# Keys in chunks of 128 and a shared rest of 64: one change to an attention and SwiGLU kernel

## The chip, the cores and the metric

The kernel runs on one core of a Trainium2 chip. The metric is the device time of one execution in microseconds (us), the median of several runs. The engines are named as in the profile: PE is TensorE's matmul row and PEld its weight loads, DVE is VectorE, ACT is ScalarE, POOL is GpSimd, and SP is SyncE, which only issues transfers here.

## The reference

Attention over 8 batches of 12 heads, 448 tokens and head size 64 comes first. Its output, as 3584 tokens of 768 values, goes through a SwiGLU block with 1536 hidden values.

```python
scores = scale * np.matmul(q, k.transpose(0, 1, 3, 2))
attn = np.exp(scores - np.max(scores, axis=-1, keepdims=True))
attn = attn / (np.sum(attn, axis=-1, keepdims=True) + 1e-09)
x = np.matmul(attn, v).transpose(0, 2, 1, 3).reshape(B * S, H * D)
g = x @ w_gate
out = (g / (1.0 + np.exp(-g)) * (x @ w_val)) @ w_out
```

Inputs and output are float32. The kernel computes in float16 with float32 sums. It leaves the maximum out of the softmax, since the scores are small.

## The kernel before

**Attention, by pairs of heads.** There are 48 pairs. A pair's 448 keys lie as four chunks of 112 (P = 112, NC = 4). qk(pr, c) at L192 multiplies one chunk of transposed keys with all 448 queries, once for each head. The two matmuls use 64 rows each (the head size), and write the two halves of one buffer of the pool ps_s, which has three buffers. One exp on ACT (L205) turns the buffer into E, 112 x 896 in float16.

**Products, by two pairs.** Three products follow for every two pairs, that is four heads. sums(p0) (L236) multiplies E with ones and gives the row sums, and pv(p0, t) (L213) for t = 0 and 1 gives the two halves of the output values. Each product is 16 matmuls of 32 output columns: four chunks by four heads, one head in each quarter of the output rows. It needs one buffer of the pool ps_f, which has two. DVE empties that buffer: after sums by a copy to ssb (L255), with four reciprocals later (L258), and after pv by a multiplication with the reciprocals, which writes X (scaled, L232).

**FFN.** The tokens are cut into eight blocks of 384 and 512 in turn. ffn1_steps (L277) gives, for each of 12 slices of the hidden size, gp (a ps_s buffer, gate) and vp (a ps_f buffer, value), six matmuls each. ACT forms tanh of gp (L289), DVE forms t (L301) and then hts (L304), which frees vp. ffn2_steps (L309) gives op, 12 matmuls of 384 columns in a ps_f buffer for 128 tokens and half of the output. ACT copies op to osb (L334), and SP stores it. mm (L268) splits a matmul into four of 32 output columns while tiled is set, so that work beside a product has the same form as the product.

**The order around the change.** The whole order is written out by hand. After six pairs the loop over plan (L502) begins. Each visit has some score chunks (two up to pair 8, then three) and up to two due products. A visit issues its scores first, then the first product, then its share of the FFN (run_fv and run_o), with the second product before run_o or, in the first blocks, before all of the FFN share. Reciprocals wait in the list deferred and are issued one by one between FFN steps; a new product issues those that are left. Buffers of a pool are handed out in turn, and an instruction waits until the readers of the buffer it takes are done.

**Loads.** POOL issues the loads of q, k, v and the weights, which turn float32 into float16. load_qk16 (L112) brings two pairs, load_v (L121) three. From pair 11 on, prep (L144) copies a pair's q and k together on POOL (L154), and SP issues a transposing DMA (L157) into qkT. Earlier pairs are transposed on PE. Visits in which a pair begins call prep for the pair three ahead and load_qk16 for six ahead. wo, the output weights, are loaded in two halves by load_w, issued when pairs 6 and 7 begin.

Of the kernel before, what the change touches and what calls it, by code (L numbers as in the profile page):

```python
# [10 lines left out]
FP32 = mybir.dt.float32  # L11
# [10 lines left out]
RB = 5  # L22
FIRST = 6
TILED = 8
WIDE = 8


@with_exitstack
def kernel(
# [46 lines left out]
    ps_s = ctx.enter_context(tc.tile_pool(name="ps_s", bufs=3, space=PSUM))  # L76
    ps_f = ctx.enter_context(tc.tile_pool(name="ps_f", bufs=2, space=PSUM))

    ones = consts.tile([P, 32], FP16, name="ones")
    warm = consts.tile([128, 512], FP16, name="warm")  # L80
    ident = consts.tile([P, P], FP16, name="ident")
    wgv = {}
# [13 lines left out]
    E = {}  # L96
    R = {}
    X = {}

    def dummy(n):  # L100
        wp = ps_f.tile([128, 512], FP32, tag="f", name="wp")
# [9 lines left out]

    def load_qk16(pr, n=2):  # L112
        q16 = raws.tile([P, 4, NC, D], FP16, tag="rq", bufs=RB, name="q16")
        k16 = raws.tile([P, 4, NC, D], FP16, tag="rk", bufs=RB, name="k16")
        for dst, src in ((q16, q), (k16, k)):
            flat = src.rearrange("b h s d -> (b h) s d")[2 * pr : 2 * pr + 2 * n]
            nc.gpsimd.dma_start(dst[:, 0 : 2 * n], flat.rearrange("h (p c) d -> p h (c d)", c=NC))  # L117
        for i in range(n):
            raw[pr + i] = (q16[:, 2 * i : 2 * i + 2], k16[:, 2 * i : 2 * i + 2])

    def load_v(g, lo=0, hi=2 * GP):  # L121
        b = g // GPB
        h0 = (g % GPB) * 2 * GP
        if lo == 0:
            v16[g] = raws.tile([P, 2 * GP, NC, D], FP16, tag="vt", bufs=3, name="vt")
        nc.gpsimd.dma_start(  # L126
            v16[g][:, lo:hi],
            v[b, h0 + lo : h0 + hi].rearrange("h (p c) d -> p h (c d)", c=NC),
        )

    def load_w(kind, i):
        if kind == "o":
# [9 lines left out]
        nc.gpsimd.dma_start(dst[:], src)  # L142

    def prep(pr):  # L144
        rq, rk = raw[pr]
        if pr == 0 or pr >= NPE:
            qk16 = attp.tile([P, 2, NC, 2, D], FP16, tag="qk16", bufs=3)
            for t, src in enumerate((rq, rk)):
                dst = qk16[:, 1 - t].rearrange("p c h d -> p h c d")
                if pr == 0:  # L150
                    nc.vector.tensor_copy(dst[:, 0], src[:, 0])
                    nc.scalar.activation(dst[:, 1], src[:, 1], AF.Copy)
                else:
                    nc.gpsimd.tensor_copy(dst, src)  # L154
        qkT[pr] = attp.tile([128, 2 * NC, P], FP16, tag="qkT", name="qkT", bufs=5)
        if pr >= NPE:
            nc.sync.dma_start_transpose(  # L157
                qkT[pr][:], qk16[:].rearrange("p t c h d -> p (t c h d)")
            )
            return None  # L160

        def turn0():
            for t in range(2):
                tp = ps_s.tile([128, 2, 512], FP32, tag="s", name="tp")
                for c in range(NC):
                    for hx in range(2):
                        nc.tensor.matmul(
                            tp[ts(hx, 64), c // 2, ds(c % 2 * P, P)],
                            lhsT=qk16[:, 1 - t, c, hx],
                            rhs=ident[:],  # L170
                            start=True,
                            stop=True,
                        )
                dst = qkT[pr][:, ts(1 - t, NC)].rearrange("p (a c) q -> p a (c q)", a=2)
                nc.vector.tensor_copy(dst[:, 0], tp[:, 0, 0 : 2 * P])
                nc.scalar.activation(dst[:, 1], tp[:, 1, 0 : 2 * P], AF.Copy)

        def turn():
            if pr < FIRST + 2:
                tp = ps_s.tile([128, 2 * NC, 256], FP16, tag="s", name="tp")  # L180
            else:
                tp = ps_f.tile([128, 2 * NC, 128], FP16, tag="f", name="tp")
            for t in range(2):
                for c in range(NC):
                    for hx in range(2):
                        src = raw[pr][t][:, hx, c, :]
                        nc.tensor.transpose(tp[ts(hx, 64), (1 - t) * NC + c, 0:P], src, ident[:])
            nc.vector.tensor_copy(qkT[pr][:], tp[:, :, 0:P])

        return turn if pr else turn0  # L190

    def qk(pr, c):  # L192
        if c == 0:
            E[pr] = ep.tile([P, NC, 2, S], FP16, tag="E", name="E")
        t = qkT[pr]
        s = ps_s.tile([128, 2, 512], FP32, tag="s")
        for hx in range(2):
            nc.tensor.matmul(  # L198
                s[:, hx, 0:S],
                lhsT=t[ts(hx, 64)].rearrange("p c q -> p (c q)")[:, c * P : c * P + 128],  # L200
                rhs=t[ts(hx, 64), NC:, :].rearrange("p c q -> p (c q)"),
                start=True,
                stop=True,
            )
        nc.scalar.activation(E[pr][:, c], s[0:P, :, 0:S], AF.Exp, scale=sm_scale)  # L205

    def qk_half(pr, half, between=None):
        for c in (2 * half, 2 * half + 1):
# [1 line left out]
            if between and c % 2 == 0:  # L210
                between()

    def pv(p0, t):  # L213
        acc = ps_f.tile([128, 512], FP32, tag="f", name="acc")
        for c in range(NC):
            for j in range(4):
                g, r = divmod(p0 + j // 2, GP)
                nc.tensor.matmul(  # L218
                    acc[ts(j, 32), 0:S],
                    lhsT=v16[g][:, 2 * r + j % 2, c, :].rearrange("p (d t) -> p t d", t=2)[:, t],  # L220
                    rhs=E[p0 + j // 2][:, c, j % 2, :],
                    start=(c == 0),
                    stop=(c == NC - 1),
                )
        return acc

    def scaled(p0, t, acc):
# [8 lines left out]
    def sums(p0, wide=False):  # L236
        if wide:
            acc = ps_s.tile([128, 2, 512], FP32, tag="s", name="acc")[:, 0]
        else:
            acc = ps_f.tile([128, 512], FP32, tag="f", name="acc")  # L240
        for c in range(NC):
            for j in range(4):
                nc.tensor.matmul(  # L243
                    acc[ts(j, 32), 0:S],
                    lhsT=ones[:],
                    rhs=E[p0 + j // 2][:, c, j % 2, :],
                    start=(c == 0),
                    stop=(c == NC - 1),
                )
        R[p0] = attp.tile([128, S], FP32, tag="R", bufs=2, name="R")  # L250
        return acc

# [108 lines left out]
    with tc.manual_schedule():  # L361
        load_qk32(0)
        nc.vector.memset(warm[:], 0.0)
        nc.vector.memset(ones[:], 1.0)
        load_qk16(1, 1)
        make_identity(nc, ident)
        load_qk16(2, 1)
# [38 lines left out]
        def add_block(i, visits):  # L406
            f1, f2, n = block(i)
            oq.extend(ffn2_wait)
            ffn2_wait.clear()
            fvq.extend([(f1, NCB * n / 2400.0)] * NFB)  # L410
            own = [(f2, NFB * OH / 2400.0)] * (2 * (n // 128))
            (oq if i == 0 else ffn2_wait).extend(own)
            count.update(visits=visits, fv=NFB, o=len(oq), at=0, more=NFB - visits)
# [56 lines left out]
        load_table("exp_and_others")  # L470
        halves = [pv(p4, t) for t in range(2)]

        queue = []
        for p0 in range(FIRST, NPAIR, 2):
            for kind, m in (("sums", 8), (0, 11), (1, 14)):
                queue.append((NC * p0 + m, kind, p0))
        plan = []
        g = FIRST * NC
        last = NPAIR * NC
        while g < last or queue:  # L480
            n = 2 if g < WIDE * NC else 3
            todo = []
            while queue and queue[0][0] <= g and len(todo) < 2:
                todo.append(queue.pop(0))
            plan.append(([divmod(x, NC) for x in range(g, min(g + n, last))], todo))
            g += n
        adds = {0: 0}
        for x, (_, todo) in enumerate(plan):
            for _, kind, p0 in todo:
# [3 lines left out]
        def product(kind, p0):  # L493
            if kind == "sums":
                pop_deferred(99)
                deferred.extend(recips(p0, sums(p0)))
            else:
                pop_deferred(99)
                scaled(p0, kind, pv(p0, kind))

        carry = 0.0
        for x, (chunks, todo) in enumerate(plan):  # L502
# [9 lines left out]
            for pr in entered:  # L512
                if NPE <= pr + 3 < NPAIR:
                    prep(pr + 3)
                if pr % 2 == 0 and 14 <= pr + LA < NPAIR:
                    load_qk16(pr + LA)
                if (pr + 2) % GP == GP - 1 and 4 <= (pr + 2) // GP + 1 < NGRP:
                    load_v((pr + 2) // GP + 1)
            for pr, c in chunks:
                if c == 2 and pr < NPE - 2:  # L520
                    prep(pr + 2)()
            if todo:
                product(*todo[0][1:])
            if x in adds and x > 0:
                add_block(adds[x], end - x)
            for pr in entered:
                for w in wq.pop(pr, []):
                    emit(w)
            tiled[0] = bool(todo) and (not chunks or chunks[0][0] >= TILED)
            if adds[max(y for y in adds if y <= x)] < 2:  # L530
                for item in todo[1:]:
                    product(*item[1:])
# [55 lines left out]
```

## Time and profile before

| | us |
|---|---|
| median of 13 runs | 461.54 |
| lowest and highest run | 458.82 and 463.68 |
| the profiled execution, whole | 459.12 |
| its span, first to last instruction | 457.3 |
| busy time of the exps of the scores (L205) | 161.8 |
| busy time of POOL | 104.3 |

The profile shows one execution. Its busy times are those of that execution, and a sum made from them has to be set against 459.12, not against the median. Matmuls overlap each other, so the mean duration of one is longer than the distance from one start to the next; the distance between starts shows what PE needs. The granted clock of PE was 0.998 over the span. DMA is busy in nearly all of the first 80 us and much less after 120 us.

### The profile page before, as it was taken

The numbers are of one execution on the slowest core, as the hardware profiler recorded it, in microseconds if no ns is written. First come the engines' busy times: TensorE is split into PE (matmuls) and PEld (weight loads), VectorE is DVE, ScalarE is ACT, GpSimd is POOL, SyncE is SP. The second block draws the span as 40 slices with busy tenths as digits, with TensorE's granted clock in tenths as the row PEclk, the third lists the DMA queues.
The fourth block names the chain that finished last, engine by engine and source line by source line (L and its number), as shares of the span: only waits on it lengthen the run. The fifth ranks groups of instructions, "written<-read, shape, count | busy, mean of one in ns | idle before, by whom it ended". The sixth has DMA issues, their size and how long they took to land.

```text
span 457.3 us, 17024 instructions
## 1 busy us (share of the span) xinstructions
PE 448.2 (98%) x7807; PEld 249.6 (55%) x7807; DVE 239.2 (52%) x371; ACT 240.2 (53%) x353; POOL 104.3 (23%) x164
## 2 busy tenths in 40 slices
PE   8899999999999999999999999999999999999996
PEld 3355555444466665455566666555555666544564
DVE  2765764666764545745546546645466356354200
ACT  6986657666554655546364555544555551222222
POOL 8554704435160042301323013310200000000000
PEclk9999999999999999999999999999999999999999
DMA  9999999999984176940839358953222010100133
GB/s 135 195 200 201 184 179 165 149 198 138 105 106 64 43 110 101 151 83 9 127 61 129 57 79 128 120 51 76 33 57 56 20 54 20 56 0 1 36 103 105
DMA packets 82056, 44.42 MB, mean 97 GB/s; under 512 B 36672, under 2 KB 78528, under 8 KB 81984
## 3 DMA queue, kind: packets, MB, share of 16 engines
q0 software_dynamic: 42368, 23.37, 40.6%
q1 hardware_dynamic: 39520, 19.92, 25.4%
q8 instruction: 61, 1.00, 0.9%
q14 instruction: 11, 0.09, 0.1%
q10 hardware_dynamic: 96, 0.05, 0.0%
HBM read 47.19 MB, written 11.01 MB: 127 GB/s over the span
## 4 chain that ended last, share of the span: by engine, by line
PE 79%; DMA 14%; POOL 3%; DVE 2%; issue 1%; ACT 1%; POOLq 0%; DVEq 0%
PE gp L273 17%; PE vp L273 17%; PE op L273 15%; PE acc L218 7%; PE s L198 6%; PE op L270 6%; DMA q<-in_q_dram 6%; DMA wv<-in_moe_w_val_dram 5%; PE gp L270 4%; PE vp L270 4%; PE acc L243 3%; DMA wg<-in_moe_w_gate_dram 2%; DMA qkT<-qk 1%; POOL q L117 1%; POOL k L117 1%
## 5 line engine op out<-in xcount | busy, mean ns | idle before, releaser
L205 ACT ACTIVATE E<-s 112x896 f16<-112x896 f32 x192 | 161.8, 921 | 21.4 <-PE s L198 21.0
L273 PE MATMUL gp<-X,wg 128*32 128x384 f16 (+1 forms) x1848 | 100.7, 351 | 0.0
L273 PE MATMUL vp<-X,wv 128*32 128x384 f16 (+1 forms) x1848 | 100.5, 351 | 0.1
L301 DVE SCALAR_TENSOR_TENSOR t<-sg,gp 128x384 f32<-128x384 f32 (+1 forms) x96 | 59.1, 616 | 78.7 <-ACT sg L289 78.7
L289 ACT ACTIVATE sg<-gp 128x384 f32<-128x384 f32 (+1 forms) x96 | 52.8, 550 | 71.1 <-PE gp L273 45.7
L334 ACT ACTIVATE osb<-op 128x384 f32<-128x384 f32 (+1 forms) x57 | 27.7, 485 | 117.7 <-PE op L273 93.9
L273 PE MATMUL op<-wo,hts 128*32 128x384 f16 x1968 | 87.1, 326 | 0.8 <-DMA wo<-in_moe_w_out_dram 0.6
L273 PEld LDWEIGHTS <-wg 128*32 128x32 f16 x1848 | 53.0, 96 | 35.6 <-issue 0.2
L258 DVE RECIPROCAL R<-ssb 128x112 f32<-128x112 f32 x92 | 71.9, 822 | 0.8
L273 PEld LDWEIGHTS <-wv 128*32 128x32 f16 x1848 | 52.9, 97 | 33.8 <-issue 0.3
L273 PEld LDWEIGHTS <-hts 128*32 128x32 f16 x1968 | 56.9, 97 | 26.1 <-DMA wo<-in_moe_w_out_dram 1.0
L304 DVE SCALAR_TENSOR_TENSOR hts<-t,vp 128x384 f16<-128x384 f32 (+1 forms) x96 | 59.6, 621 | 10.4 <-DVE t L301 0.5
L232 DVE TENSOR_TENSOR X<-acc,R 128x448 f16<-128x448 f32 x48 | 29.7, 624 | 56.8 <-PE acc L218 53.7
L198 PE MATMUL s<-qkT 64*128 64x448 f16 x384 | 50.4, 353 | 2.8 <-ACT E L205 1.5
L126 POOL DMA_DIRECT2D vt<-in_v_dram x16 | 12.3, 772 | 157.7 <-PE acc L218 156.6
L218 PE MATMUL acc<-E,vt 112*32 112x448 f16 x768 | 45.1, 355 | 0.0
L154 POOL COPY qk<-q 112x512 f16<-112x512 f16 x37 | 22.9, 619 | 47.6 <-DMA qkT<-qk 28.7
L198 PEld LDWEIGHTS <-qkT 64*128 64x128 f16 x384 | 14.9, 94 | 33.3 <-issue 26.3
L255 DVE COPY ssb<-acc 128x448 f32<-128x448 f32 x23 | 14.4, 624 | 32.3 <-PE acc L243 32.2
L270 PE MATMUL op<-wo,hts 128*128 128x384 f16 (+1 forms) x192 | 29.6, 316 | 0.0
L218 PEld LDWEIGHTS <-vt 112*32 112x32 f16 x768 | 16.6, 96 | 23.3 <-issue 14.7
L270 PE MATMUL gp<-X,wg 128*128 128x512 f16 (+1 forms) x114 | 25.5, 360 | 0.0
(38 smaller groups left out, 204.7 us busy)
## 6 DMA issues: line engine op xcount, KB each, us to landing
vt<-in_v_dram POOLq DMA_DIRECT2D x16, 336.0 KB, 7.5
q<-in_q_dram POOLq DMA_DIRECT2D x22, 224.0 KB, 7.3
k<-in_k_dram POOLq DMA_DIRECT2D x22, 224.0 KB, 8.4
out_dram<-osb SPq DMA_DIRECT2D x7, 336.0 KB, 3.1
wg<-in_moe_w_gate_dram POOLq DMA_DIRECT2D x8, 288.0 KB, 11.3
wv<-in_moe_w_val_dram POOLq DMA_DIRECT2D x8, 288.0 KB, 11.5
wo<-in_moe_w_out_dram POOLq DMA_DIRECT2D x2, 1152.0 KB, 22.8
out_dram<-osb SPq DMA_DIRECT2D x8, 288.0 KB, 3.0
```

The costliest lines, as they stand in the source:

```text
L154: nc.gpsimd.tensor_copy(dst, src)
L198: nc.tensor.matmul(s[:, hx, 0:S], lhsT=t[ts(hx, 64)].rearrange("p c q -> p (c q)")[:, c * P : c * P + 128], rhs=t[ts(hx, 64), NC:, :].rear ...
L205: nc.scalar.activation(E[pr][:, c], s[0:P, :, 0:S], AF.Exp, scale=sm_scale)
L218: nc.tensor.matmul(acc[ts(j, 32), 0:S], lhsT=v16[g][:, 2 * r + j % 2, c, :].rearrange("p (d t) -> p t d", t=2)[:, t], rhs=E[p0 + j // 2][: ...
L232: nc.vector.tensor_tensor(X[kk][:, hp + t, ts(bb, S)], acc[:, 0:S], R[p0][:], ALU.mult)
L258: lambda i=i: nc.vector.reciprocal(rt[:, ts(i, P)], ssb[:, ts(i, P)]) for i in range(4)
L270: nc.tensor.matmul(dst, lhsT=lhsT, rhs=rhs, start=start, stop=stop)
L273: nc.tensor.matmul(dst[ts(j, 32), :], lhsT=lhsT[:, ts(j, 32)], rhs=rhs, start=start, stop=stop)
L289: nc.scalar.activation(sg[:, 0:n], gp[:, 0:n], AF.Tanh, scale=0.5)
L301: nc.vector.scalar_tensor_tensor(t1[:, 0:n], sg[:, 0:n], 1.0, gp[:, 0:n], ALU.add, ALU.mult)
L304: nc.vector.scalar_tensor_tensor(hts[:, fb, 0:n], t1[:, 0:n], 0.5 * HS, vp[:, 0:n], ALU.mult, ALU.mult)
L334: nc.scalar.activation(osb[:, ds(m0, w)], op[:, 0:w], AF.Copy, scale=1.0 / HS)
```

## The change

From pair 12 on (FULL = 12) a pair's keys and values lie as three chunks of 128 and a rest of 64. The rests of the two heads lie below each other on 128 partitions. For the scores, the rests of the keys are placed in a block-diagonal tile (the other blocks are set to zero), so that one matmul over 128 rows gives the rest scores of both heads, in one buffer of ps_f, with one exp of 448 elements. In the products the fourth step of each head reads this shared rest, with values, or ones, that are zero in the rows of the other head. The number of matmuls in a product stays 16.

The loads follow: k of two pairs takes three DMAs instead of one, v of three pairs takes three and a memset, and prep has two memsets and four copies instead of two copies. load_v is issued after the visit's first product.

The plan of visits changes. Visits have two chunks up to pair 8 and three from pair 9; from pair 12 on a visit is one pair, with its rest after the first product. Products are due by visits. Where a block's last product falls in a visit, all products due are issued at once, ahead of the rest.

```diff
-WIDE = 8
+FULL = 12
-    ones = consts.tile([P, 32], FP16, name="ones")
+    ones = consts.tile([128, 3, 32], FP16, name="ones")
...
     def load_qk16(pr, n=2):
...
+        km = k16[:, 0 : 4 * 3 * D].rearrange("p (h c d) -> p h c d", h=4, c=3)
+        kr = k16[:, 4 * 3 * D : 4 * 3 * D + 2 * D].rearrange("p (i d) -> p i d", i=2)
+        nc.gpsimd.dma_start(km, kf[:, 0:SM].rearrange("h (p c) d -> p h (c d)", c=3))
+        for hx in range(2):
+            nc.gpsimd.dma_start(
+                kr[ts(hx, SR)], kf[:, SM:].rearrange("(i t) p d -> t p i d", t=2)[hx]
+            )
...
     def load_v(g):
...
+        nc.gpsimd.memset(v_rest(g), 0.0)
+        nc.gpsimd.dma_start(v_main(g), v[b, heads, 0:SM].rearrange("h (p c) d -> p h (c d)", c=3))
+        for hx in range(2):
+            nc.gpsimd.dma_start(
+                v_rest(g)[ts(hx, SR), :, hx],
+                v[b, heads, SM:].rearrange("(i t) p d -> t p i d", t=2)[hx],
+            )
...
     def prep(pr):
+        if pr >= FULL:
+            rq, km, kr = raw[pr]
+            qk16 = attp.tile([128, 2, NC, 2, D], FP16, tag="qk16", bufs=3, name="qk16")
+            nc.gpsimd.memset(qk16[96:128, 1], 0.0)
+            nc.gpsimd.memset(qk16[:, 0, 3], 0.0)
+            nc.gpsimd.tensor_copy(qk16[:, 0, 0:3].rearrange("p c h d -> p h c d"), km)
+            for hx in range(2):
+                nc.gpsimd.tensor_copy(qk16[ts(hx, SR), 0, 3, hx], kr[ts(hx, SR)])
+            nc.gpsimd.tensor_copy(qk16[0:P, 1].rearrange("p c h d -> p h c d"), rq)
+            qkT[pr] = attp.tile([128, 2 * NC, 128], FP16, tag="qkT", name="qkT", bufs=5)
+            nc.sync.dma_start_transpose(
+                qkT[pr][:], qk16[:].rearrange("p t c h d -> p (t c h d)")
+            )
+            return None
...
     def qk(pr, c):
...
+        m = 128 if full else P
+        dst = (e_main if full else e_old)(pr)[:, c]
+        nc.scalar.activation(dst, s[0:m, :, 0:S], AF.Exp, scale=sm_scale)
+
+    def qk_rest(pr):
+        s = ps_f.tile([128, 512], FP32, tag="f", name="sr")
+        mm(s[:, 0:S], lhsT=qkT[pr][:, 3], rhs=qkT[pr][:, NC:, 0:P], start=True, stop=True)
+        nc.scalar.activation(e_rest(pr), s[:, 0:S], AF.Exp, scale=sm_scale)
...
+    def reduce4(p0, acc, weights):
         for c in range(NC):
             for j in range(4):
-                g, r = divmod(p0 + j // 2, GP)
+                pr, hx = p0 + j // 2, j % 2
+                if pr < FULL:
+                    rhs = e_old(pr)[:, c, hx, :]
+                else:
+                    rhs = e_main(pr)[:, c, hx, :] if c < 3 else e_rest(pr)
                 nc.tensor.matmul(
                     acc[ts(j, 32), 0:S],
-                    lhsT=v16[g][:, 2 * r + j % 2, c, :].rearrange("p (d t) -> p t d", t=2)[:, t],
-                    rhs=E[p0 + j // 2][:, c, j % 2, :],
+                    lhsT=weights(pr, hx, c),
+                    rhs=rhs,
                     start=(c == 0),
                     stop=(c == NC - 1),
                 )
...
+        nc.vector.memset(ones[:, 0], 1.0)
+        for hx in range(2):
+            nc.vector.memset(ones[:, 1 + hx], 0.0)
+            nc.vector.memset(ones[ts(hx, SR), 1 + hx], 1.0)
...
+        visits = []
+        g = FIRST * NC
+        while g < FULL * NC:
+            n = 2 if g < 9 * NC else 3
+            visits.append([divmod(x, NC) for x in range(g, g + n)])
+            g += n
+        visits += [[(pr, c) for c in range(3)] for pr in range(FULL, NPAIR)]
+        done = {pr: x for x, chunks in enumerate(visits) for pr, _ in chunks}
+        plan = []
         queue = []
         for p0 in range(FIRST, NPAIR, 2):
-            for kind, m in (("sums", 8), (0, 11), (1, 14)):
-                queue.append((NC * p0 + m, kind, p0))
+            x = done[p0 + 1] + 1
+            step = 2 if x < len(visits) and len(visits[x]) == 2 else 1
+            queue += [(x, "sums", p0), (x + step, 0, p0), (x + step + 1, 1, p0)]
...
-            if todo:
+            if x in adds and x > 0:
+                while todo:
+                    product(*todo.pop(0)[1:])
+                add_block(adds[x], end - x)
+            elif todo:
                 product(*todo[0][1:])
-            if x in adds and x > 0:
-                add_block(adds[x], end - x)
             for pr in entered:
+                if (pr + 2) % GP == GP - 1 and 4 <= (pr + 2) // GP + 1 < NGRP:
+                    load_v((pr + 2) // GP + 1)
                 for w in wq.pop(pr, []):
                     emit(w)
-            tiled[0] = bool(todo) and (not chunks or chunks[0][0] >= TILED)
+            tiled[0] = bool(todo or x in adds) and (not chunks or chunks[0][0] >= TILED)
+            for pr in entered:
+                if pr >= FULL:
+                    qk_rest(pr)
```

## The prediction

> **What bounds the kernel now.** I read the page first, then the waits, then stretches of the timeline by engine.
>
> ```profile
> PE 448.2 (98%) x7807; PEld 249.6 (55%) x7807; DVE 239.2 (52%) x371; ACT 240.2 (53%) x353; POOL 104.3 (23%) x164
> L205 ACT ACTIVATE E<-s 112x896 f16<-112x896 f32 x192 | 161.8, 921 | 21.4 <-PE s L198 21.0
> ```
>
> TensorE is busy for 98% of the span; ScalarE, the engine that the change relieves, for 53%. So the time follows from what TensorE streams and from its gaps. The waits give one gap for each entry into the score matmuls (73 of them):
>
> ```profile
> PEld L198 <- issue: 26.3, 73, 0.7
> ```
>
> The timeline of PE alone, one visit (a turn of the loop over plan, numbered x from 0 below) of block 1, shows what an entry costs:
>
> ```profile
> 97.19 0.74 PE L198 MATMUL s<-qkT 64*128 64x448 f16 x6
> 97.86 0.94 PE L243 MATMUL acc<-E,ones 112*32 112x448 f16 x16
> 98.63 1.47 PE L273 MATMUL gp<-X,wg 128*32 128x512 f16 x24
> 99.92 1.47 PE L273 MATMUL vp<-X,wv 128*32 128x512 f16 x24
> 101.22 1.47 PE L273 MATMUL gp<-X,wg 128*32 128x512 f16 x24
> 102.51 1.47 PE L273 MATMUL vp<-X,wv 128*32 128x512 f16 x24
> 103.91 0.36 PE L198 MATMUL s<-qkT 64*128 64x448 f16 x2
> ```
>
> Starts matter here, not durations. Six groups of four 32-column matmuls take 1.295 us (99.92 to 101.22), 0.216 per 512 columns; by columns, 0.189 for 448 and 0.1625 for 384. Into the scores 102.51 to 103.91 is 1.40, so 0.105 is lost; out of them 97.19 to 97.86 is 0.67 for three chunks of 0.189, so 0.10 is lost. Product to gp is 0.77 for 0.756. Nothing else is lost: all waste beside these 0.205 us a visit is a real wait, as here:
>
> ```profile
> 130.18 1.16 PE L273 MATMUL vp<-X,wv 128*32 128x384 f16 x24
> 131.16 0.94 PE L243 MATMUL acc<-E,ones 112*32 112x448 f16 x16
> 131.59 0.55 DVE L304 SCALAR_TENSOR_TENSOR hts<-t,vp 128x384 f16<-128x384 f32 x1
> 132.20 2.13 PE L273 MATMUL op<-wo,hts 128*32 128x384 f16 x48
> ```
>
> acc to op takes 1.04 for 0.756 of columns: op needs the ps_f buffer (of two) that vp held, and VectorE gives it back at 132.14. A product's buffer comes back later still:
>
> ```profile
> 210.18 0.94 PE L218 MATMUL acc<-E,vt 112*32 112x448 f16 x16
> 211.17 0.62 DVE L232 TENSOR_TENSOR X<-acc,R 128x448 f16<-128x448 f32 x1 [1.70 <-PE acc L218]
> ```
>
> It is free 0.99 + 0.62 + about 0.07 = 1.68 us after the product's start. Last, the DMA limits two places:
>
> ```profile
> 63.30 0.94 PE L218 MATMUL acc<-E,vt 112*32 112x448 f16 x16
> 64.79 1.49 PE L273 MATMUL op<-wo,hts 128*32 128x384 f16 x32 [0.55 <-DMA wo<-in_moe_w_out_dram]
> ```
>
> ```profile
> 48.37 25.27 DMA q<-in_q_dram
> ...
> 75.50 5.88 DMA qkT<-qk
> 81.39 0.05 issue
> 81.43 0.74 PE s L198 x6
> ```
>
> The first op waits 0.73 us for w_out (1.49 less 0.756), and pair 14's scores at 81.43 follow its transposing DMA (the second fence is the chain of waits in 55 to 85 us).
>
> [...] the key and value rests write 128 B runs, which no row of before shows.
>
> **The change, part by part.**
>
> *Columns.* A pair before is 4 score chunks, after 3 chunks and a rest: the rest streams 448 columns once, like a chunk. Products keep 16 matmuls of 448. FFN work is the same. Net 0. Memsets of ones at the start: under 0.1 us each (L364 has 85 ns), beside the first loads, 0.
>
> *ScalarE.* Per pair 4 exps at 921 become 3 and one of 448 (L264, 448 wide, has 577 ns): 36 x 0.34 = 12 us less, worth 0 by itself, as TensorE is the bound. But tanh now queues behind four exps: in the stretch above it started at +2.96 us after the scores (100.15), and will at about +3.5.
>
> *Visits.* From the instruction order: visits with scores go from 58 to 46, since 8 chunks of two pairs took 2.67 visits and now take 2. 12 x 0.205 = -2.5. The rest sits between product and gp, which hides the 0.02 that gp waited there: 36 x 0.02 = -0.7. Third chunks waited 0.01 each, 24 fewer: -0.2.
>
> *w_out.* With pair 8 now in visits of two, op in visit x=8 comes after 2 chunks and one product less: 0.38 + 0.76 = 1.1 us of columns wait for later, while w_out sets the start at 64.8 as before. The key load of pair 12 is ahead of it in the queue: 512 + 256 packets instead of 448. Taking 50 and 32 ns each (on a line through the trace's median packets, 512 B at 60 and 768 B at 79 ns) and 16 engines, +0.44 us; between 0 and 1.5, as short packets are not shown. Together +1.6 (0.5, if something else already holds the visits before it, to 2.6).
>
> *Pair 14's scores.* They come at visit x=12, which by the sums here is about 85 us instead of 81.4. Its keys land some 1 to 2 us later (w_out, own packets), and POOL's queue issues four DMAs a load, each waiting for the one eight earlier, so pair 16's load, queued ahead of pair 14's copies, waits for 14's own; then two memsets and four copies (0.62 per 512 columns, so about 2.2 us instead of 1.2) and 5.9 to landing: 85.3 to 86.2. +0.9 (0 to 2.5). Later pairs are prepared three visits (about 24 us) ahead; POOL at some 4.5 us a pair stays covered, and so does SP, whose transposes stand behind out stores only. load_v moved behind the visit's first product: POOL waits for that product, and what is queued behind (the pair three on) has over two visits; 0.
>
> *The rest takes a ps_f buffer, and two buffers rotate.* Product in A, rest in B, so what follows next needs A, free at +1.68.
> - x=10, 14, 16: a second product follows; 1.68 - 0.756 - 0.189 = 0.73 each, +2.2. At x=10 op then needs B, held until the rest's exp ends at about +3.5 from the scores while op is ready at 3.1: +0.45 (0 to 0.6).
> - x=11: op follows the rest: +0.73.
> - x=12, 18, 24, 30, 36, 42: two products ahead of the rest, 1.68 - 2 x 0.756 = 0.16: +1.0.
> - x=20, 22, 32, 34, 44 (384 columns) and 26, 28, 38, 40 (512): sums after two vp, then op, as at 131.16: 5 x 0.29 + 4 x 0.36 = +2.9 (1.8 to 4); the 0.36 adds the longer L304 and the earlier end of vp. Visit 46 has one more, +0.3.
> - x=13, 15, 17: the third chunk needs gp's buffer, which VectorE reads late after the later tanh: +0.5 (0 to 1). At 103.91 before it fitted by 0.05.
>
> *Waits of before that go:* 0.17 at 81.4, two of 0.29 (132, 241), 0.42 at 352 to 354, small ones of about 0.5: -1.4.
>
> Sum: -3.4 + 1.6 + 0.9 + 2.65 + 0.7 + 1.0 + 3.2 + 0.5 - 1.4 = +5.8. The profiled execution took 459.12 us (span 457.3 and 1.8 around it), so 464.9 of that kind; it is 2.4 us below the median of the 13 runs, so 461.54 + 5.8 = 467.3.
>
> **Rivals.**
> - *The rotation costs little, and the kernel gets faster.* Place: the ps_f waits above, 8.1 us in all with the third chunks. If VectorE and ScalarE free buffers as early as TensorE asks, 5.8 - 8.1 = -2.3: 459.2. It decides once these waits come to under about 0.9 us (the rest of the sum is -2.3, and 1.4 can be told apart). For it: most ps_f hand-overs of before cost nothing. Against: 131.16 to 132.20 shows the very sequence, and 1.68 against 0.95 is not close.
> - *No change.* The 12 mode changes and the waits cancel, with w_out no later and the sums waits half: 461.5. Against: each wait has its own row.
> - *The loads lag.* 128 B and 384 B runs cost far more than I take, and POOL's chain of eight holds each later load; pairs 14 to 18 come late by 4 to 6 us more: 472. For it: DMA share is over 1.3 until 80 us. Against: it falls to 0.3 to 0.9 from 120 us.
>
> **How the numbers follow.** Forecast (463 to 469.5) 0.64, loads lag 0.14, no change 0.12, faster 0.10. This kernel's runs tell 0.3% (1.4 us) apart. Slower 0.78, same 0.12, faster 0.10. The range leaves out part of the faster case and the upper end of the lag: 461 to 471.
>
> **What would show it.** Right: 61 issue gaps instead of 73; first op near 65 us with 2 to 3 us of wait; a second product 1.7 us after the first at three visits; op 0.3 late after sums in nine visits; the last score matmul's visit later than before. Wrong: sr followed at once by acc or op, or a wait on DMA qkT in many visits.

## The result, and the profile after

The kernel after takes 465.38 us, median of 11 runs (462.34 to 467.89); the kernel before takes 461.35 in 48 runs beside them. The ratio is 1.0096, with a 95% interval of 1.0073 to 1.012: 4.4 us more (461.35 x 0.0096). The profiled execution of after took 465.38 us, its span 463.6, which is 6.3 us above the 457.3 of before.

The page of after, engines first, then the instruction queue and the row of the score exps:

```profile
PE 448.7 (97%) x7843; PEld 247.5 (53%) x7843; DVE 239.1 (52%) x375; ACT 226.1 (49%) x353; POOL 184.7 (40%) x380
...
q8 instruction: 61, 1.00, 0.9%
...
L263 ACT ACTIVATE E<-s 128x896 f16<-128x896 f32 (+1 forms) x156 | 131.4, 923 | 12.8 <-PE s L260 12.6
```

ScalarE lost 14.1 us of work (240.2 to 226.1), and POOL got 80.4 more (104.3 to 184.7). TensorE's busy time is nearly the same (448.2 and 448.7), and so the time follows from its gaps. The waits of after:

```profile
PEld L260 <- issue: 21.8, 61, 0.7
...
POOL vt L156 <- DMA wo<-in_moe_w_out_dram: 3.6, 1, 3.6
...
PE op L350 <- issue: 2.3, 1, 2.3
...
PE acc L284 <- DVE X L311: 1.7, 3, 0.6
...
PE vp L350 <- issue: 0.8, 1, 0.8
...
PE op L350 <- DVE hts L381: 0.7, 4, 0.2
```

There are 61 entries into the scores instead of 73. The three waits of a product for X are the three second products of the prediction. What it did not have are the two waits of matmuls on "issue", that is, waits for nothing that the profile shows. The timeline of PE around a second product (visit 14), around a visit in which op follows sums (visit 20), and at the first op (columns: start, duration, what, and in brackets the idle time before it):

```profile
97.47 0.94 PE L284 MATMUL acc<-E,vt 128*32 128x448 f16 x16
98.23 0.36 PE L350 MATMUL sr<-qkT 128*32 128x448 f16 x4
99.14 0.94 PE L284 MATMUL acc<-E,ones 128*32 128x448 f16 x16 [0.54 <-DVE X L311]
```

```profile
149.12 0.93 PE L284 MATMUL acc<-E,ones 128*32 128x448 f16 x16
150.17 1.16 PE L350 MATMUL op<-wo,hts 128*32 128x384 f16 x24
```

```profile
61.80 0.94 PE L284 MATMUL acc<-E,ones 112*32 112x448 f16 x16
62.56 1.64 PE L350 MATMUL op<-wo,hts 128*32 128x384 f16 x36
```

From 97.47 to 99.14 is 1.67 us for 0.945 of columns: 0.72 lost. From 149.12 to 150.17 is 1.05 for 0.756: 0.29 lost. At 61.80 to 62.56 nothing is lost (0.76 for 0.756); the wait for w_out that before had there is gone.

The new gap, in the timeline of PE and in windows of one microsecond (busy share of PE, PEld, DVE, ACT and POOL with counts, then granted clock, DMA share, GB/s):

```profile
285.75 3.10 PE L350 MATMUL op<-wo,hts 128*32 128x384 f16 x72
291.18 1.78 PE L350 MATMUL op<-wo,hts 128*32 128x384 f16 x24 [2.33 <-issue]
292.90 1.30 PE L260 MATMUL s<-qkT 64*128 64x448 f16 x6
294.13 1.33 PE L284 MATMUL acc<-E,vt 128*32 128x448 f16 x16
295.30 0.93 PE L284 MATMUL acc<-E,ones 128*32 128x448 f16 x16
```

```profile
289.00:290.00 1.00, 0.00 (x0) 0.00 (x0) 0.00 (x0) 0.00 (x0) 0.00 (x0) 1.00 0.03 1
290.00:291.00 1.00, 0.00 (x0) 0.00 (x0) 0.00 (x0) 0.00 (x0) 0.00 (x0) 1.00 0.01 0
...
293.00:294.00 1.00, 1.00 (x6) 0.18 (x5) 0.00 (x0) 0.99 (x2) 0.00 (x0) 0.50 0.00 0
```

In the middle of op's matmuls every engine stands still, and then TensorE runs at half clock: 292.90 to 295.30 takes 2.40 us for two groups that need 0.67 and 0.756. The gap costs 2.5 us, the slow stretch some 1.6; a smaller one of 0.93 lies at 247.7. Before's profiled execution has one such gap, of 0.1 us, at 301.08. What is it that TensorE has none of? The DMA view of after for 278.2 to 288.6 us and for 288.6 to 291.2 (queue, packets, MB, share of 16 engines):

```profile
q0 software_dynamic: 1241, 0.45, 45.0%
q1 hardware_dynamic: 1156, 0.65, 39.8%
```

```profile
q0 software_dynamic: 39, 0.00, 3.1%
q8 instruction: 1, 0.02, 3.0%
q1 hardware_dynamic: 60, 0.01, 2.5%
```

The queue "instruction" (q8) moves TensorE's program, going by the count: 61 packets for 2 x 7843 matmuls and weight loads are 257 instructions each, 61 for 2 x 7807 in before are 256, and 30 for 2 x 3847 in e5 below are 256 again. So a packet is read here as a block of 256 instructions. Matmuls of a quarter width and 384 columns start every 0.1625 / 4 = 0.041 us and have a weight load each, so a block lasts about 128 x 0.041 = 5.2 us, an estimate from these starts. Through the 10.4 us from 278.2 to 288.6, two blocks long, a burst of stores, loads and a transposing DMA ran and no packet of q8 came (one of q14, the other instruction queue, did). The packet came as the burst ended, and TensorE, dry since about 288.6, went on at 291.18.

That these gaps stand between two blocks can be counted. Two windows of after run from the start of the span into the two gaps:

```profile
0.00:248.60 248.60, 240.58 (x4444) 129.73 (x4444) 142.39 (x226) 145.06 (x216) 149.70 (x302) 1.00 0.98 131
0.00:290.00 290.00, 280.45 (x5339) 154.01 (x5340) 163.19 (x260) 163.46 (x247) 166.19 (x338) 1.00 0.94 125
```

Matmuls and weight loads together are 8888 and 10,679. These are 1791 apart, and with one semaphore instruction of TensorE between them, which the windows leave out, 1792, which is seven times 256. e3 and e6 below show the same distances at other places of the work.

### The profile page after: what moved, and what is told of

It reads as the page before. It is cut to its first block, busy times and chain, and to the rows that moved or that the text cites. A ratio compares the mean times of both kernels' runs of the same rounds, so it can differ in the third digit from the quotient of the medians.

```text
span 463.6 us, 17335 instructions
## 1 busy us (share of the span) xinstructions
PE 448.7 (97%) x7843; PEld 247.5 (53%) x7843; DVE 239.1 (52%) x375; ACT 226.1 (49%) x353; POOL 184.7 (40%) x380
## 4 chain that ended last, share of the span: by engine, by line
PE 88%; DVE 5%; ACT 3%; issue 1%; DMA 1%; SPq 0%; DVEq 0%; ACTq 0%
PE gp L350 18%; PE op L350 18%; PE vp L350 16%; PE acc L284 11%; PE s L260 7%; PE op L347 6%; PE gp L347 5%; PE vp L347 5%; ACT E L263 2%; DVE t L378 2%; PE sr L350 2%; DVE hts L381 1%; ACT sg L366 1%; DVE R L335 1%; DMA rk<-in_k_dram 1%
## 5 line engine op out<-in xcount | busy, mean ns | idle before, releaser
L263 ACT ACTIVATE E<-s 128x896 f16<-128x896 f32 (+1 forms) x156 | 131.4, 923 | 12.8 <-PE s L260 12.6
L350 PE MATMUL vp<-X,wv 128*32 128x384 f16 (+1 forms) x1824 | 99.5, 351 | 0.8 <-issue 0.8
L350 PE MATMUL gp<-X,wg 128*32 128x384 f16 (+1 forms) x1824 | 99.2, 351 | 0.0
L350 PE MATMUL op<-wo,hts 128*32 128x384 f16 x1968 | 87.2, 328 | 4.4 <-issue 2.3
L350 PEld LDWEIGHTS <-hts 128*32 128x32 f16 x1968 | 56.1, 97 | 32.7 <-issue 7.8
L350 PEld LDWEIGHTS <-wv 128*32 128x32 f16 x1824 | 50.4, 97 | 36.4 <-issue 1.1
L350 PEld LDWEIGHTS <-wg 128*32 128x32 f16 x1824 | 50.8, 97 | 34.6
L153 POOL MEMSET vt<- 128x384 f16 x12 | 5.0, 418 | 114.4 <-PE acc L284 114.4
L284 PE MATMUL acc<-E,vt 128*32 128x448 f16 (+1 forms) x768 | 45.6, 357 | 0.2 <-DMA vt<-in_v_dram 0.2
L260 PE MATMUL s<-qkT 64*128 64x448 f16 x312 | 41.9, 357 | 2.1 <-ACT E L263 1.5
L284 PEld LDWEIGHTS <-vt 128*32 128x32 f16 (+1 forms) x768 | 16.9, 97 | 23.9 <-issue 15.3
L347 PE MATMUL op<-wo,hts 128*128 128x384 f16 (+1 forms) x192 | 29.6, 316 | 0.0
L347 PE MATMUL gp<-X,wg 128*128 128x512 f16 (+1 forms) x120 | 26.7, 358 | 0.2 <-DVE t L378 0.2
L260 PEld LDWEIGHTS <-qkT 64*128 64x128 f16 x312 | 12.2, 94 | 27.3 <-issue 21.8
L347 PE MATMUL vp<-X,wv 128*128 128x512 f16 (+1 forms) x120 | 26.6, 358 | 0.0
L284 PE MATMUL acc<-E,ones 128*32 128x448 f16 (+1 forms) x384 | 22.6, 353 | 2.1 <-DVE X L311 1.7
```

The lines of the kernel that those rows point to most:

```text
L153: nc.gpsimd.memset(v_rest(g), 0.0)
L260: nc.tensor.matmul(s[:, hx, 0:S], lhsT=lhsT, rhs=rhs, start=True, stop=True)
L263: nc.scalar.activation(dst, s[0:m, :, 0:S], AF.Exp, scale=sm_scale)
L284: nc.tensor.matmul(acc[ts(j, 32), 0:S], lhsT=weights(pr, hx, c), rhs=rhs, start=(c == 0), stop=(c == NC - 1),)
L347: nc.tensor.matmul(dst, lhsT=lhsT, rhs=rhs, start=start, stop=stop)
L350: nc.tensor.matmul(dst[ts(j, 32), :], lhsT=lhsT[:, ts(j, 32)], rhs=rhs, start=start, stop=stop)
```

## The experiments

Two theories stood against each other. W: the 4.4 us are the waits of the prediction, ps_f above all. F: they are mostly late instruction packets, and the rotation (the two buffers of ps_f, taken in turn) is a lesser part. Each comparison uses runs of before on the same chip in the same hour; before's median moved there between 459.5 and 461.7.

**e1: products first.** After, with all due products ahead of the rest, so that the rest no longer takes the buffer of the second one.

```diff
-            if x in adds and x > 0:
+            had = bool(todo)
+            if (x in adds and x > 0) or (chunks and chunks[0][0] >= FULL):
                 while todo:
                     product(*todo.pop(0)[1:])
-                add_block(adds[x], end - x)
             elif todo:
                 product(*todo[0][1:])
+            if x in adds and x > 0:
+                add_block(adds[x], end - x)
```

> The changed kernel with every product that is due issued ahead of the rest from pair 12 on (all work kept). Theory W (the extra time is mostly waits for the two rotating ps_f buffers): three waits of 0.74 before a second product become 0.15 before the rest, nine waits of 0.28 to 0.34 before op become 0.15 before the rest, the wait of op at x=10 stays at 0.4 to 0.5: 3.1 us less than the changed kernel, about 462.3 median. Theory F (the extra time is mostly TensorE running out of instructions, the gaps that the trace calls issue): the same waits vanish from the trace, but the median stays above 464, since the gaps of 1 to 2.5 us stay.

Measured: 461.34 us (22 runs) against 461.26; ratio 1.0017 (0.9998 to 1.0035). The same visit in the timeline of PE:

```profile
97.02 0.94 PE L284 MATMUL acc<-E,vt 128*32 128x448 f16 x16
97.79 0.93 PE L284 MATMUL acc<-E,ones 128*32 128x448 f16 x16
98.69 0.37 PE L350 MATMUL sr<-qkT 128*32 128x448 f16 x4
98.88 1.48 PE L350 MATMUL gp<-X,wg 128*32 128x512 f16 x24
```

The 0.72 between the products is gone, and 0.14 comes ahead of the rest (97.79 to 98.69 is 0.90). The order of the products is worth some 4 us (3.6 by the two ratios), 3.1 of which W priced. F, which expected more than 464, misses here too. Gaps on issue of 1.1 and 1.4 us are still there in the profiled execution. So W's waits are real, and they aren't all that the change brought.

**e2: no rest loads.** After, without the DMAs of the key and value rests; these rests count as zero, so the last 64 keys of each head enter with scores and values of zero.

```diff
-        for hx in range(2):
-            nc.gpsimd.dma_start(
-                kr[ts(hx, SR)], kf[:, SM:].rearrange("(i t) p d -> t p i d", t=2)[hx]
-            )
+        nc.gpsimd.memset(kr, 0.0)
...
         nc.gpsimd.dma_start(v_main(g), v[b, heads, 0:SM].rearrange("h (p c) d -> p h (c d)", c=3))
-        for hx in range(2):
-            nc.gpsimd.dma_start(
-                v_rest(g)[ts(hx, SR), :, hx],
-                v[b, heads, SM:].rearrange("(i t) p d -> t p i d", t=2)[hx],
-            )
```

> The changed kernel without the loads of the rests of k and v (their rows are zero instead, so part of the attention is left out); TensorE, ACT and DVE do what they did. 36 + 24 DMAs and 9,200 packets of 128 B are gone. Theory W: no change against the changed kernel, 465.4 within 0.6 us. Theory F, with short packets delaying the fetch of instructions: 1.5 to 3 us less, 462.4 to 463.9, and fewer gaps called issue.

Measured: 462.89 us (11 runs), ratio 1.004 (1.0018 to 1.0061), 2.5 us below after. The instruction sequence of TensorE is that of after, and its ps_f waits stayed (2.2 us before second products, as in after). The gaps on issue shrank to 0.6 and 0.2 us, without half clock. W alone, which expected no change, falls. And the wait for w_out is back, in the timeline of PE:

```profile
62.21 0.94 PE L276 MATMUL acc<-E,ones 112*32 112x448 f16 x16
64.52 1.80 PE L342 MATMUL op<-wo,hts 128*32 128x384 f16 x39 [1.37 <-DMA wo<-in_moe_w_out_dram]
```

The two profiles agree with the time: fetch gaps and half clock take 0.8 us here and 5.0 in after (2.5 + 1.6 + 0.93), and the wait for w_out adds 1.55 (64.52 less 62.21, less 0.756), which makes 2.65 us less.

**e3: short runs in before.** Before, with the keys and values from pair 12 on loaded in two DMAs of 256 B runs each instead of one of 512 B: 16,608 more packets and 30 more DMAs.

```diff
+            for e in range(2):
+                nc.gpsimd.dma_start(dst[:, 0 : 2 * n, ts(e, 2)], flat[:, :, ts(e, 2 * D)])
...
+        for e in range(2):
+            nc.gpsimd.dma_start(v16[g][:, lo:hi, ts(e, 2)], src[:, :, ts(e, 2 * D)])
```

> The kernel before, with k and v from pair 12 on loaded by two DMAs each in runs of 256 B instead of 512 B (same bytes and results, 16,000 packets more, 30 DMAs more). Theory F, with short packets delaying the fetch of instructions: 1.5 to 3 us slower than before, with gaps called issue of 1 us or more in the trace. Theory W: the same as before within 0.6 us.

Measured: 461.26 us (22 runs), as before itself; ratio 0.9995 (0.9975 to 1.0016). A miss for F as it stood then: more and shorter packets do not by themselves move the median. The kernel isn't free of late fetches, though. Its profiled execution, one of its longest (463.18 us), has gaps on issue of 0.6, 1.1 and 0.7 us: in a product, ahead of gp and in op. Counted as above, they stand behind 2495, 2751 and 10,687 instructions, which is 1 and 31 blocks of 256 apart. Before has runs as long (up to 463.92 us), but none of those was profiled, so whether such gaps make them long is not shown.

**e4: half an exp in before.** Before, with half of the fourth chunk's exp from pair 12 on left out; the second head's part is set to one by POOL.

```diff
-        nc.scalar.activation(E[pr][:, c], s[0:P, :, 0:S], AF.Exp, scale=sm_scale)
+        w = 1 if pr >= 12 and c == 3 else 2
+        nc.scalar.activation(E[pr][:, c, 0:w], s[0:P, 0:w, 0:S], AF.Exp, scale=sm_scale)
+        if w == 1:
+            nc.gpsimd.memset(E[pr][:, c, 1], 1.0)
```

> The kernel before, with the exp of the fourth chunk done for one of two heads only from pair 12 on (36 times 0.34 us less on ScalarE; the other half of E is set to one by POOL, so this part of the computation is left out). Both theories: ScalarE is not the bound, so the same as before within 0.6 us. A rival in which ScalarE's work is on the path says up to 12 us less.

Measured: 460.4 us (22 runs) against 461.26; ratio 1.0002 (0.9979 to 1.0025), so the same, with ScalarE at 228.5 us instead of 240.2. The relief that the change brings to ScalarE is worth nothing, as the prediction had it.

**e5: fewer instructions.** After, with the FFN's matmuls at full width (only the rest stays split in four): 3847 matmuls instead of 7843.

```diff
-TILED = 8
+TILED = 99
...
             for pr in entered:
                 if pr >= FULL:
+                    tiled[0] = True
                     qk_rest(pr)
+                    tiled[0] = False
```

> The changed kernel with the FFN matmuls left whole in every visit (128 output columns, not four times 32), so that TensorE has 7,700 instructions instead of 15,700; the rest stays split. Each visit changes mode once more (0.1 us, about 46 visits), and each second product behind FFN work twice more (12 x 0.2): about 7 us added. Theory F (TensorE runs out of instructions, 4 to 5 us of the changed kernel's median): these gaps vanish, so about 467, with the runs within 1 us of each other and no gap called issue over 0.5 us in the middle. Rival (the spread of the runs and the gaps have nothing to do with the number of instructions): about 472, with a spread of 5 us as before.

Measured: 464.23 us (6 runs), ratio 1.0103 (1.0083 to 1.0122), beside runs of before with 459.61. The page:

```profile
PE 451.2 (98%) x3847; PEld 225.1 (49%) x3847; DVE 239.2 (52%) x375; ACT 225.8 (49%) x353; POOL 184.3 (40%) x380
...
q8 instruction: 30, 0.49, 0.4%
```

Half the instructions, half the packets, and no gap on issue above 0.15 us in the middle of the kernel, with all the loads of after in place; the runs lie within 1.6 us of each other (463.92 to 465.52), those of after within 5.6. For F it is what it asked for: the gaps go with the rate of instructions. The time shows less: in ratio to before it is no lower than after's (1.0096), so something takes what the gaps gave back, some 3.5 us by the profiled executions (a span of 462.1 against after's 463.6 without the 5.0). The changes between full and quarter width are the likely place: PEld stands on issue at 62 entries into the FFN's matmuls (L347 and L350 below), where after has 24. Their 7 us in the expectation were an estimate from the 0.10 and 0.105 us that before loses around the scores. The waits of e5:

```profile
PEld L347 <- issue: 19.1, 55, 0.5
...
PEld L350 <- issue: 1.8, 7, 0.4
```

**e6 and e8: additional loads in before.** Before, with the 60 DMAs of the rests added; nothing reads what they bring. e6 (below) has the 128 B runs of the change, e8 runs of 512 B and four times the bytes.

```diff
+        if pr >= 12:
+            kx = raws.tile([128, 2, D], FP16, tag="kx", bufs=4, name="kx")
+            kf = k.rearrange("b h s d -> (b h) s d")[ds(2 * pr, 4)]
+            for hx in range(2):
+                nc.gpsimd.dma_start(
+                    kx[ts(hx, 64)], kf[:, 384:].rearrange("(i t) p d -> t p i d", t=2)[hx]
+                )
```

> The kernel before, which also loads from pair 12 on the rests of k and v as the changed kernel does, into tiles that nothing reads (60 DMAs and 9,200 packets of 128 B more; all work kept). Theory F with the loads of the rests as the cause: 2 to 3 us slower than before, 463.3 to 464.3. Rival (the gaps come from where the loads, transposes and stores of the changed kernel's visits fall together, not from the loads of the rests by themselves): the same as before within 0.7 us.

> As e6, the kernel before with 60 more loads that nothing reads, as many packets as in e6, but of 512 B instead of 128 B (four times the bytes; all work kept). If the short runs of the rests are what holds up the fetch: the same as before within 0.7 us. If it is the additional DMAs on POOL's queue, whatever their length: at least the 3 us of e6 slower than before.

Measured: e6 462.96 us (7 runs), ratio 1.0072 (1.004 to 1.0105), 3.3 us above before's 459.61; e8 464.46 (22 runs), ratio 1.0055 (1.003 to 1.008). The timeline of PE of e6 has the gap of after, in a kernel without any of the change's work on TensorE:

```profile
301.05 2.12 PE L287 MATMUL op<-wo,hts 128*32 128x384 f16 x48
305.82 1.12 PE L212 MATMUL s<-qkT 64*128 64x448 f16 x6 [2.66 <-issue]
```

This gap stands behind 11,199 counted instructions, two blocks behind e3's last. The execution is one of e6's longest (465.5 us). The additional DMAs cost 3.3 us by themselves, where the change costs 4.4 in all. e8's ratio can't be told from e6's, so nothing says that long runs are cheaper; but e8's loads share one buffer where e6's have four, and so may wait for each other, which makes it no pure test of the length. e3 added more packets than e6 (16,608 against 10,176) without moving the median, so the count of packets by itself is not it.

**e7: the rest behind gp.** e1, and the rest one step later still, behind the first gp of the visit (whose buffer is of ps_s), or behind op where the visit has none.

```diff
+            had = bool(todo)
+            if (x in adds and x > 0) or (chunks and chunks[0][0] >= FULL):
...
             for pr in entered:
                 if pr >= FULL:
-                    qk_rest(pr)
+                    rests.append(pr)
...
+                while rests:
+                    qk_rest(rests.pop(0))
```

> The kernel of e1 with the rest moved behind the first gp of the visit (behind op where a visit has no gp); all work kept. The ps_f waits of e1 (2.8 us before the rest and 1.25 us before op behind it) vanish but for 0.2, so 3.9 us less than e1: about 457.5 median, and the first version that is faster than the kernel before by over 0.5%. Theory F: gaps called issue of 2 us or more stay in the trace. If the waits only move to vp (whose buffer the rest then holds), the time stays at 461.

Measured: 456.61 us (9 runs), ratio 0.9924 (0.9898 to 0.9949): faster than both kernels. The same visit in the timeline of PE:

```profile
96.44 0.94 PE L284 MATMUL acc<-E,vt 128*32 128x448 f16 x16
97.21 0.93 PE L284 MATMUL acc<-E,ones 128*32 128x448 f16 x16
97.97 1.47 PE L350 MATMUL gp<-X,wg 128*32 128x512 f16 x24
99.26 0.36 PE L350 MATMUL sr<-qkT 128*32 128x448 f16 x4
99.45 1.47 PE L350 MATMUL vp<-X,wv 128*32 128x512 f16 x24
```

Every start follows the one before by its columns (0.77, 0.76, 1.29, 0.19). Of 7.25 us of ps_f waits 0.47 are left. The fetch gaps are not touched: 0.7 and 2.8 us in this execution.

**e9: the rests on SP's queue.** e7, with the rests loaded as float32 by SP and turned into float16 by POOL copies.

```diff
-        kr = k16[:, 4 * 3 * D : 4 * 3 * D + 2 * D].rearrange("p (i d) -> p i d", i=2)
+        kr = k16[:, 4 * 3 * D :].bitcast(FP32).rearrange("p (i d) -> p i d", i=2)
...
-            nc.gpsimd.dma_start(
+            nc.sync.dma_start(
```

> The kernel of e7 with the rests of k and v loaded as float32 by SP's queue (runs of 256 B written), and turned into float16 by POOL's copies, of which v has two more per three pairs; all work kept. If the rests' loads in POOL's queue hold up the fetch, the gaps shrink and it is 1 to 3 us faster than e7 (454 to 456, ratio to before 0.985 to 0.990). If the additional DMAs do it on whatever queue: as e7 within 0.7 us.

Measured: 457.83 us (8 runs), ratio 0.9929 (0.9897 to 0.9961), the same as e7. The gaps on issue shrank to 0.5 us, and the wait for w_out came back, larger, as the timeline of PE has it:

```profile
61.78 0.94 PE L291 MATMUL acc<-E,ones 112*32 112x448 f16 x16
65.11 1.17 PE L357 MATMUL op<-wo,hts 128*32 128x384 f16 x20 [2.39 <-DMA wo<-in_moe_w_out_dram]
```

TensorE ran at half clock from 65.8 us on, for 3.4 us (granted clock 0.50 in each microsecond from 66 to 69, 0.90 in the ones beside them). What the fetch gave, this took. That POOL's queue is worse for the fetch than SP's isn't shown by this, with one profiled execution of each.

**e10: w_out earlier.** e9, with the first half of w_out issued ahead of the keys of pair 12.

```diff
-            4: [("g", 3), ("v", 3), ("qk", 12)],
-            6: [("V", 3), ("o", 0)],
+            4: [("g", 3), ("v", 3), ("o", 0), ("qk", 12)],
+            6: [("V", 3)],
```

> The kernel of e9 with the load of the first half of w_out issued ahead of the loads of pair 12 and of the third group's successor (when pair 4 begins, not pair 6); all work kept. In e9 op waited 2.57 us for w_out at 62.4 us, and the clock then stood at half for about 3.4 us. If that wait is what kept e9 from gaining on e7, both go: 3 to 4.5 us less than e9, about 453.5, ratio to before 0.982 to 0.986. If DMA in the first 70 us is full anyway, the wait only moves to the keys of pair 12: as e9.

Measured: 464.55 us (6 runs), ratio 1.0104 (1.0069 to 1.0138). A miss: the wait only moved. In the timeline of PE:

```profile
78.42 0.38 PE L357 MATMUL sr<-qkT 128*32 128x448 f16 x4
83.53 1.30 PE L267 MATMUL s<-qkT 64*128 64x448 f16 x6 [4.74 <-DMA qkT<-qk]
```

Now the later keys are late. What is put forward in the first 80 us pushes back something else that TensorE needs there.

## Why the prediction was right, and where it wasn't

It said 467.3 us, 5.8 more, in 461 to 471, and slower. The time came out at 465.38, 4.4 more. Sign and size are right, but only part of the sum is why. All figures here are starts of PE less columns, as in the prediction.

- *Columns and visits*: right. 61 entries instead of 73; what entries lose from 62 us on went from 10.8 to about 8.2 us, close to the predicted -2.5. The 0.02 ahead of gp is gone too (it was 0.014, 0.77 less 0.756, so 36 of them are 0.5 and not 0.7).
- *ScalarE worth nothing*: right, and e4 shows it by itself.
- *The rotation of ps_f*: right almost to the digit. Second products 0.74, 0.71 and 0.74 (0.73 each predicted); op of visit 10 0.40 (0.45); op of visit 11 0.71 (0.73); six visits with two products ahead of the rest 0.88 in sum (1.0); op behind sums 0.28 and 0.34 (0.29 and 0.36). In all 7.25 us against 7.6. e1 and e7 take these waits away, and the time goes with them.
- *Third chunks of visits 13, 15 and 17*: +0.5 predicted, 0 measured. *Pair 14's scores*: +0.9 predicted, 0 measured. Both were within the bounds given.
- *w_out*: wrong in sign. The step put +1.6 us there, since w_out would land no earlier and the work to hide it is less; the 0.7 us of before went away instead. It assumed "w_out sets the start at 64.8 as before". The timelines of POOL, of after and then one line of before, show what was different:

```profile
48.25 2.05 POOL L172 DMA_DIRECT2D wo<-in_moe_w_out_dram  x2 [1.25 <-issue]
...
61.80 0.64 POOL L156 DMA_DIRECT2D vt<-in_v_dram  x1 [3.55 <-DMA wo<-in_moe_w_out_dram]
...
64.24 0.61 POOL L183 COPY qk<-q 112x512 f16<-112x512 f16 x1
70.80 0.75 POOL L120 DMA_DIRECT2D q<-in_q_dram  x1 [5.95 <-DMA wo<-in_moe_w_out_dram]
```

```profile
54.33 0.62 POOL L154 COPY qk<-k 112x512 f16<-112x512 f16 x1
```

The prediction knew that a DMA of POOL waits for the one eight earlier (the load at 61.80 is the eighth behind the first half of w_out, and waited 3.55 us for it; the next, at 70.80, waited 5.95 for the second half), and used it only for what would be late. It also holds back traffic: the last copy of pair 13 ended at 64.85 (64.24 + 0.61) instead of 54.95 in before (54.33 + 0.62), so its transposing DMA could not run beside w_out, and w_out's first half, issued 3.0 us later than in before, landed 13.3 us after its issue instead of 19.5: at 61.5 us. In e2 POOL isn't held there and the rests aren't loaded; w_out takes 19.5 us again, and the wait is back. The other runs go the same way: where POOL is held (e1, e3, e5, e6, e7) it takes 14.1 to 16.3 us, and where it isn't (e9) 19.7. So the hold and the early landing go together; which of the DMAs that are moved slows w_out, no run told apart.

These three steps are 3.7 us too much (2.3 + 0.9 + 0.5), the rotation 0.35. The sum of the prediction's own steps is then 5.8 - 4.05 = 1.75 us, and the profiled executions come near: 463.6 less 5.0 of fetch gaps with their half clock is 458.6, before's 457.3 less 0.1 is 457.2, which is 1.4 apart.

- *What was missed*: the fetch. No step, and no rival, had TensorE run out of instructions. The rival "the loads lag" named the added DMAs as the danger, but through late keys, and no run shows that in after. At the median the fetch makes up what is left, by subtraction 4.4 - 1.75 = 2.7 us. e6, with these DMAs alone, measured +3.3; e2, without them, -2.5 against after; e5, with half the instructions, has no such gaps. That TensorE stands for want of its next block is the reading of the counts (gaps 256, 1792 and 7936 instructions apart); that the additional DMAs bring this about, beside a dense stream of instructions, is that of e2 and e6. Why the queues let the packet wait, and why e3's DMAs left the median where it was, stays open.
- *Two readings of before* were loose, without weight in the sum: the DMA share is 1.13 in the first 20 us and over 1.3 only behind them, and from 120 us on it lies between 0.0 and 0.98 and not between 0.3 and 0.9.

So the rotation and the visits were foreseen, and the right size of the whole was luck beyond that: two errors cancel, 3.7 us of waits that did not come, and 2.7 us of a cause that was not thought of.

## What to carry to other kernels

An operation put between two others takes a buffer, and with two buffers that rotate it makes the next one wait for the one before last: place it where the next buffer comes from another pool (here order alone took the ratio from 1.0096 to 0.9924). Cutting matmuls into four makes four times the instructions, and these come by DMA too (queue q8: 61 packets in after, 30 in e5): look for gaps on "issue" in the middle of a run of matmuls, and count whether they are whole blocks of 256 instructions apart. Additional DMAs beside such a stretch can cost time there (3.3 us in e6); whether moving bursts of loads, stores and transposing DMAs away from it helps, no run here tried. When a queue is held by its own DMAs, ask also what that keeps out of the way of others.

## What the hardware showed unexpectedly

TensorE stood dry for 0.5 to 2.8 us in the middle of a row of independent matmuls, not only in after and the kernels with the added loads (e1, e6, e7, e9, e10) but also in e2 and e3, while the instruction queue took 0.9% of the DMA engines' time in after.

A gap of this length can be followed by half clock, and need not be. By the idle times in the timelines, 2.33 us in after, 2.39 in e9 and 2.66 in e6 were followed by it: the granted clock was 0.50 in after from 291.56 to 294.97, 3.41 us long, in e9 from 66 to 69 us, and in e6 from 307 to 308. In e7 2.66 us were not; its windows behind the gap (which ends at 286.71) stay at full clock:

```profile
285.00:286.00 1.00, 0.00 (x0) 0.00 (x0) 0.00 (x0) 0.00 (x0) 0.00 (x0) 1.00 0.03 1
286.00:287.00 1.00, 0.29 (x8) 0.23 (x11) 0.00 (x0) 0.00 (x0) 0.00 (x0) 1.00 0.00 0
287.00:288.00 1.00, 1.00 (x26) 0.47 (x16) 0.00 (x0) 0.08 (x1) 0.00 (x0) 1.00 0.09 16
```

In after the fall did not come with the end of the gap either: from 291.18 to 291.56 TensorE was busy again, at a clock of 1.00. So the idle time alone does not tell the cases apart, as e6 and e7 have the same 2.66 us. What does was not shown by these four traces.
